# First scores from 256 keys, x's later chunks transposed by DMA, spaced late weights and a rearranged end in a gated attention kernel

## The chip, the core and the metric

One core of a Trainium2 chip runs the kernel. The metric is the device time of one launch in microseconds, the median of several runs; less is better. The engines are TensorE (PE; the profile keeps its weight loads apart as PEld), VectorE (DVE), ScalarE (ACT), GpSimd (POOL) and SyncE (SP, which here only issues DMAs). Each engine takes its instructions in program order and waits at semaphores.

## The reference

All inputs and the output are bf16. S is 2048, D 640, H 32 heads of 20, F 1536.

```python
x = A_x
g = _sigmoid((x * gate_w).sum(-1, keepdims=True))
a = _A_ref(x, A_wqkv, A_wo)             # 32-head softmax attention, then @ wo
b = _B_ref(x, B_w1, B_b1, B_w2)         # (h * tanh(softplus(h))) @ w2 with h = x @ w1 + b1
return g * a + (1 - g) * b
```

## The kernel before

Four heads make a pack, 512 queries a chunk; a pack with a chunk is a group, 32 groups in all. In a group each of 16 key tiles (128 keys) gives four score tiles of 128x512, one per head, computed by four row strips of PE (`score`). A step `S2,0` in the text issues two such tiles into two banks of PSUM, `x` the exponential of them on ACT (two or three tiles in one instruction). A key tile can instead be taken by DVE: `d` takes it, `D` issues one of its four score tiles, and `power_of` (L556) makes the exponential as an integer shift of bits; POOL makes two shifted copies of the finished set (L586), so that such a key tile takes three PV steps where an exponential of ACT takes one (a variant, `two`, takes two). A PV step `V` is four matmuls into the accumulator bank. `normalise` divides at the end of a group, through a transpose on DVE.

Everything else is cut into chains: products that are run in pieces (`C` begins a chain, `F` runs one piece) between the blocks of scores, with an evacuation (`y`) on DVE. Chains make the transposes of x (`transpose_chain`), K of the first pack (`first_k_chain`), the other Q and K (`dense_chain`), V (`v_chain`), the MLP and the final projection (`wo_chain`). The text `ORDER` is the program order of all this, written out by hand for all 32 groups; the numbers behind `C` count chains sorted by their due times, so the text changes wherever the chains do. Other letters: `q`, `k`, `b`, `o` loads that SP issues, `p` POOL's shifts, `m` the Mish activation, `H` four matmuls without effect on the result, `e` the gate, `v` the scaled copies of V.

At the head, x's chunk 0 comes in four DMAs (L444), two from SP and two from ACT. PE transposes it (L1159), the copies out of PSUM go to DVE and ACT in turn (L1165, L1167). The weights of the first pack's Q and K are padded from 20 to 32 columns per head by DVE (`pad_copy`, L500); into the 12 free columns of K's weights goes `w_top` (L1171), so that the first pack's K product also makes the last columns of K for `store_top`. One fill matmul (L1175) follows. Then K and Q of chunk 0 are computed, 512 columns each (L1184), and copied out (L1194, L1192), and the ordered text begins. SP's queue holds, in this order, x chunk 0, the K weights, w_top, x chunk 1, the gate's weights, x chunk 2, a weight strip, x chunk 3, a strip, `wv`, b1, w1, two strips, w1, all of w2, and then what the text issues.

At the end, the four row tiles of the last query chunk are finished in PSUM: pack 6, then a product with the identity that adds what lies in `R`, then pack 7 when `normalise` has its output; copies and DMAs out follow.

Of the kernel before, what the change touches and what calls it, by code (L numbers as in the profile page):

```python
# [9 lines left out]
P = 128  # L10
# [3 lines left out]
BF16 = mybir.dt.bfloat16  # L14
# [5 lines left out]
S2,0 S2,2 C1,6 F x C2,5 F y1 x C3,4 F y2 S2,0 y3 C4,6 F x S3,2 y4 C5,5 F F F F x F F F F F F F F F F F F S2,0  # L20
F F S3,2 x F F C0,6 F F y5 x y6 F y7 F y8 y9 F S2,0 y10 V0,-1 x V1,-1 V2,-1 C6,6 F F F F F V3,-1 C7,5 F y11
C8,4 F y12 S2,0 S2,2 q1 C9,6 F y13 x C10,5 F y14 C11,4 F F x F F y15 F S2,0 F F F F x F F F S2,2 F F F F x F
S2,0 S2,5 F F F x y16 C12,3 F y17 y18 F y19 F y20 F x S3,0 F V4,-1 x V5,-1 y21 V6,-1 C13,6 F S3,3 y22 C14,2 F
x S2,0 y23 C15,6 F C16,2 F x y24 S3,3 y25 V7,-1 C17,6 F x F F F F F F F F F S2,0 F F F F x F S3,2 F F F F F
C18,5 F x F y26 y27 F y28 S2,0 y29 y30 F F x S2,2 y31 V8,-1 V9,-1 x V10,-1 d1,0,1 S2,0 S2,4 d1,1,0 D1,15,0,6
d1,2,0 d1,3,0 x C19,3 F y32 F F F x S3,0 D1,15,3,6 F y33 V11,-1 x S2,4 y34 C20,6 F F F F F F F F F F F x F
S3,0 D1,14,0,3 F F F y35 F F x F F F S2,4 y36 C21,3 F y37 y38 F y39 y40 e0 F v0 y41 F x S3,0 D1,15,1,6 q2 y42
V12,-1 y43 F V13,-1 x V14,-1 y44 S2,4 D1,14,3,6 C22,3 F y45 F F x F S2,0 D1,15,2,2 V15,-1 y46 F x F F S2,4
D1,13,0,6 y47 F p1,4 F F x C23,2 F F y48 F S2,0 F y51 F x S2,4 D1,13,3,6 y52 F y49 F y50 F F F x V0,-1 S2,0
D1,14,1,3 V1,-1 y53 x p2,-1 V15,0 S2,4 y55 C24,6 F y56 x F y57 F S2,0 D1,14,2,2 y54 d1,4,0 F x S2,3 D1,12,0,5  # L30
y58 F V2,-1 y59 x V15,1 p3,5 S2,0 D1,13,1,2 y60 V3,-1 V14,0 x y61 p4,0 S2,3 D1,12,3,5 C25,6 V14,1 y62 F x S2,0
D1,13,2,2 d2,1,0 F y63 F x S3,3 F p5,5 F x V4,-1 S2,0 D1,12,2,2 y64 V14,2 V13,0 y65 V5,-1 p6,0 x V13,1 S3,3
D1,12,1,6 d2,5,0 V6,-1 y66 C26,2 F x F F V13,2 F S2,0 D1,11,0,6 p7,2 F F y67 F x F q3 S2,3 D1,11,1,5 p8,0
V12,0 y68 F F x S2,0 D1,11,3,6 V7,-1 y69 V12,1 y70 x V12,2 y71 S2,2 D1,11,2,5 D2,15,1,4 d2,0,0 V8,-1 y72 x
C27,6 F F S2,0 F y73 p9,2 F F x F S2,2 D2,15,2,5 F F y74 F p10,3 F x S2,0 D2,15,0,4 V11,0 y75 V9,-1 y76 x
V11,1 y77 S2,2 D2,14,1,6 D2,14,2,5 V11,2 y78 x V10,-1 S2,0 D2,15,3,4 d2,2,0 y80 C28,6 F x F S2,2 y79 V0,-1 x
y81 F S2,0 D2,14,0,5 F y82 p11,3 y83 F x S2,2 D2,13,1,4 V1,-1 y85 V15,0 p12,4 x S2,0 D2,14,3,5 y86 d2,6,0
V15,1 C29,6 F y87 x F S2,2 D2,13,2,4 V15,2 y84 F F x y88 p13,1 F S2,0 D2,13,0,5 F F y89 F x F S2,2 D2,12,1,4
p14,3 F V2,-1 y90 V14,0 x S2,0 D2,13,3,5 y91 d3,4,0 C30,4 F F y92 F x F y93 F S2,2 D2,12,2,6 F F y94 F x F
S2,0 D2,12,0,5 V3,-1 y95 F x V14,1 S2,2 D2,11,1,6 y96 p15,1 V14,2 y97 V4,-1 x y98 S2,0 D2,12,3,5 d3,3,0 V13,0  # L40
y99 V5,-1 x S3,2 D2,11,2,6 p16,-1 V13,1 y100 V6,-1 x V12,0 p17,1 S2,0 D2,11,0,5 V13,2 y101 C32,6 F F p18,0 x F
S3,2 D2,11,3,5 d3,5,0 F y102 x F V7,-1 V12,1 y103 S2,0 D3,15,1,5 p19,1 V12,2 y104 V8,-1 x S3,2 D3,15,0,6 V11,0
p20,0 y105 V11,1 x S2,0 D3,15,2,5 V9,-1 y106 C31,6 F F F x S3,2 D3,14,1,5 V11,2 y107 F x F S2,0 y108 V10,-1
# [12 lines left out]
D4,12,3,6 y156 F F x V7,-1 V8,-1 S2,0 y157 H p34,-1 V13,0 y158 x S3,2 D5,15,0,6 C46,5 F y159 F x F F S2,0
D4,12,2,6 F y160 V13,1 x V9,-1 S2,2 D4,12,1,4 y161 d5,1,0 V10,-1 C48,6 F x y162 S2,0 D5,15,2,5 F y163 p35,2 F
x S2,2 D5,15,1,4 V11,-1 y164 F x p36,4 S2,0 D5,15,3,5 d5,5,0 F y165 d5,6,1 V12,0 x V12,1 S3,2 y166 p37,0 V12,2
x C47,5 F S2,0 D5,14,0,6 y167 F p38,2 F y168 F x F y169 S3,2 y170 V0,-1 V15,0 x S2,0 D5,14,1,6 y171 V15,1 q7
q8 y172 V1,-1 V15,2 C49,5 F x S3,2 D5,14,3,6 F y173 F x F F S2,0 D5,14,2,6 y174 d6,0,0 V2,-1 V3,-1 x S3,2 y175  # L60
D5,13,0,5 C50,6 F p39,2 x y176 F F F F S2,0 D5,13,2,5 y177 p40,3 V4,-1 x V14,0 y178 S3,2 D5,13,1,6 V14,1 y179
V5,-1 x S2,0 D5,13,3,5 d6,1,0 V14,2 y180 C51,6 F F F x S3,2 D5,12,2,5 p41,2 F y181 F x V6,-1 V13,0 p42,3 y182
S2,0 D5,12,0,5 V13,1 y183 C52,6 F x S2,2 D5,12,3,4 F y184 F x F S2,0 D5,12,1,5 d6,2,0 F y185 x V7,-1 S3,2
V13,2 y186 p43,4 V8,-1 x S2,0 D6,15,1,5 V9,-1 y188 C53,6 F F F x y187 S3,2 D6,15,0,5 q9 F F x S2,0 y189 V10,-1
p44,-1 V12,0 y190 C54,5 F F x F S2,2 D6,14,0,4 V11,-1 y191 F x F S2,0 D6,15,2,6 y192 V12,1 C55,4 F y193 x S2,2
D6,14,1,5 F y194 F x S2,0 D6,15,3,6 y195 d6,3,0 F F y197 x V0,-1 S2,2 D6,13,0,5 y198 V1,-1 p45,4 x V15,0 S2,0
D6,14,2,6 y199 C56,4 F p46,5 y200 F x S2,2 D6,13,1,5 F y196 y201 F x S2,0 D6,14,3,6 d6,0,0 F y202 V15,1 x y203
# [1273 lines left out]
```

## Time and profile before

| | us |
|---|---|
| runs shown (median, lowest, highest) | 696.98, 696.91, 697.25 |
| profiled execution, its own time | 697.02 |
| span in the profile | 695.2 |
| granted TensorE clock, mean | 0.998 |
| first score matmul, first exponential starts | 10.04, 10.47 |
| last exponential starts | 685.67 |
| DMA traffic | 40.46 MB |

The page of the profile gives busy times by engine, the chain of work that ended last, and groups of instructions. A line in order of time reads: start, length, engine, line of the program, operation, output <- input, shape, count, and in brackets the idle time before it and what ended that. A matmul's length includes the way through the array, so matmuls that follow each other overlap in it.

### The profile page before, as it was taken

The numbers are of one execution on the slowest core, as the hardware profiler recorded it, in microseconds if no ns is written. First come the engines' busy times: TensorE is split into PE (matmuls) and PEld (weight loads), VectorE is DVE, ScalarE is ACT, GpSimd is POOL, SyncE is SP. The second block draws the span as 40 slices with busy tenths as digits, with TensorE's granted clock in tenths as the row PEclk, the third lists the DMA queues.
The fourth block names the chain that finished last, engine by engine and source line by source line (L and its number), as shares of the span: only waits on it lengthen the run. The fifth ranks groups of instructions, "written<-read, shape, count | busy, mean of one in ns | idle before, by whom it ended". The sixth has DMA issues, their size and how long they took to land.

```text
span 695.2 us, 24441 instructions
## 1 busy us (share of the span) xinstructions
PE 680.5 (98%) x10325; PEld 240.0 (35%) x10325; DVE 582.0 (84%) x1009; ACT 676.6 (97%) x665; POOL 339.6 (49%) x334
## 2 busy tenths in 40 slices
PE   8999999999999999999999999999999999999997
PEld 4433333332323343333333222222234333343333
DVE  4488868888799888788898999988989988888896
ACT  5899999999999999999999999999999999999996
POOL 5025443435365434544547555554643565545543
PEclk9999999999999999999999999999999999999999
DMA  9612132313211212112031214232222121143221
GB/s 249 194 15 46 32 75 52 58 51 85 50 26 33 67 37 40 27 38 56 24 83 36 43 32 90 44 67 57 37 63 81 22 50 29 41 74 61 58 58 48
DMA packets 125613, 40.46 MB, mean 58 GB/s; under 512 B 91136, under 2 KB 124944, under 8 KB 125504
## 3 DMA queue, kind: packets, MB, share of 16 engines
q1 hardware_dynamic: 123904, 38.38, 24.7%
q8 instruction: 80, 1.31, 0.8%
q10 hardware_dynamic: 1600, 0.53, 0.3%
q14 instruction: 29, 0.24, 0.1%
HBM read 23.61 MB, written 12.79 MB: 52 GB/s over the span
## 4 chain that ended last, share of the span: by engine, by line
PE 78%; ACT 15%; DVE 3%; issue 3%; DMA 1%; SPq 0%; DVEq 0%; ACTq 0%
PE Sp L1033 26%; PE Sp L1068 26%; PE Sp L633 24%; ACT E L1051 11%; ACT big L840 3%; DVE T L556 2%; DMA w_top<-in_A_wqkv_dram 1%; PE Sp L1284 0%; ACT L1051 0%; PE Sp L1184 0%; DVE VD L538 0%; DVE big L819 0%; DVE T L1111 0%; PE Sp L643 0%; DVE bt L864 0%
## 5 line engine op out<-in xcount | busy, mean ns | idle before, releaser
L1051 ACT ACTIVATE E<-Sp 128x1024 bf16<-128x1024 f32 (+1 forms) x650 | 645.5, 1175 | 5.1 <-PE Sp L1033 4.0
L586 POOL INT64_ADD T<-T x320 | 330.4, 1043 | 340.6 <-DVE T L556 195.8
L556 DVE TENSOR_SCALAR T<-Sp 128x512 int16<-128x512 f32 x640 | 425.0, 685 | 76.9 <-PE Sp L1033 67.3
L1033 PE MATMUL Sp<-qT,kT 32*128 32x512 bf16 x2048 | 260.4, 383 | 6.2 <-ACT E L1051 3.0
L1033 PEld LDWEIGHTS <-kT 32*128 32x128 bf16 x2048 | 71.5, 91 | 240.5 <-issue 236.0
L1068 PE MATMUL Sp<-E,VA 128*21 128x512 bf16 x1408 | 133.9, 383 | 0.0
L1068 PE MATMUL Sp<-T,VD 128*21 128x512 bf16 x1252 | 117.4, 382 | 0.2
L633 PE MATMUL Sp<-w_sb,big 128*32 128x320 bf16 x1536 | 74.2, 301 | 0.6 <-DVE T L556 0.5
L633 PE MATMUL Sp<-xT,w1t 128*32 128x512 bf16 x960 | 73.4, 383 | 0.2
L1068 PEld LDWEIGHTS <-VA 128*21 128x21 bf16 x2048 | 45.5, 90 | 63.3 <-issue 54.2
L1068 PE MATMUL Sp<-T,VA 128*21 128x512 bf16 x640 | 62.4, 381 | 0.0
L633 PE MATMUL Sp<-xT,ws 128*32 128x512 bf16 x720 | 52.3, 381 | 0.2 <-ACT E L1051 0.2
L633 PEld LDWEIGHTS <-big 128*32 128x32 bf16 x1536 | 35.0, 95 | 28.0 <-issue 19.6
L1068 PEld LDWEIGHTS <-VD 128*21 128x21 bf16 x1252 | 30.8, 90 | 39.1 <-issue 32.7
L819 DVE TENSOR_SCALAR big<-Sp,b1f 128x512 bf16<-128x512 f32 x48 | 35.6, 741 | 1.5 <-PE Sp L633 1.1
L633 PE MATMUL Sp<-wv,xT 128*32 128x81 bf16 (+2 forms) x960 | 33.3, 257 | 0.4 <-DVE st L721 0.2
L633 PE MATMUL Sp<-wo_sb,od 128*32 128x320 bf16 (+1 forms) x608 | 28.9, 301 | 0.6 <-DVE T L556 0.6
L633 PEld LDWEIGHTS <-w1t 128*32 128x32 bf16 x960 | 20.1, 95 | 26.3 <-issue 19.4
L721 DVE CAST st<-Sp 128x512 bf16<-128x512 f32 x36 | 24.7, 685 | 5.3 <-PE Sp L633 5.2
L633 PEld LDWEIGHTS <-xT 128*32 128x32 bf16 x960 | 19.1, 96 | 12.8 <-issue 9.2
L777 DVE CAST VA<-Sp 128x80 bf16<-128x80 f32 (+2 forms) x48 | 16.2, 373 | 8.2 <-PE Sp L633 8.2
L633 PEld LDWEIGHTS <-ws 128*32 128x32 bf16 x720 | 16.8, 95 | 17.7 <-issue 10.0
(75 smaller groups left out, 206.1 us busy)
## 6 DMA issues: line engine op xcount, KB each, us to landing
w1t<-in_B_w_dram SPq DMA_DIRECT2D x24, 320.0 KB
q_dram<-st SPq DMA_DIRECT2D x20, 128.0 KB
b_dram<-bt SPq DMA_DIRECT2D x16, 160.0 KB
bl<-b_dram SPq DMA_DIRECT2D x16, 160.0 KB
out_dram<-ot SPq DMA_DIRECT2D x16, 160.0 KB
qT<-q_dram SPq DMA_DIRECT2D x124, 20.0 KB
o_dram<-T SPq DMA_DIRECT2D x120, 20.0 KB
kT<-k_dram SPq DMA_DIRECT2D x28, 80.0 KB
```

Source lines behind the costliest of these rows:

```text
L556: nc.vector.tensor_scalar(out=dst.bitcast(I16), in0=src, scalar1=inv_sqrt_dh * LOG2E * 128.0, scalar2=127.0 * 128.0 + (BETA2 if two else B ...
L586: nc.gpsimd.int64_add(dst[:, :].bitcast(I64), src[:, :].bitcast(I64), n * 0x0001000100010001)
L633: nc.tensor.matmul(out_[k : k + 32], lhsT=lhsT[:, k : k + 32], rhs=rhs, tile_position=(0, k), **kw)
L721: nc.vector.tensor_copy(out=res["st"][:, :], in_=ps[:, :])
L777: nc.vector.tensor_copy(out=VA[:, sts[i], h0 : h0 + nh, 0:DH], in_=ps[:, i, 0:n].rearrange("p (h d) -> p h d", d=DH),)
L819: nc.vector.tensor_scalar(out=big[:, pair_of(c, ft), (ft % 2) * QC : (ft % 2 + 1) * QC], in0=ps[:, :], scalar1=b1f[:, ft : ft + 1], scalar ...
L840: nc.scalar.activation(v, v, ACT.Mish)
L1033: nc.tensor.matmul(ps_cols, lhsT=kT[p][32 * t_ : 32 * t_ + 32, j * P : (j + 1) * P], rhs=qT[G][32 * t_ : 32 * t_ + 32, :], tile_position=( ...
L1051: nc.scalar.activation(E[:, x : x + n, :], allb[:, k0 : k0 + n, :], ACT.Exp, scale=inv_sqrt_dh,)
L1068: nc.tensor.matmul(acc[32 * t_ : 32 * t_ + DH + 1, :], lhsT=lhsT, rhs=rhs, start=(pv_done[G] == 0), stop=(pv_done[G] == pv_total[G] - 1), ...
```

## The change

- Head: the Q weights are loaded by SP and the K weights by ACT's queue (exchanged). Both pad copies go to ACT, after its copy of tile 1, which is now its only one of four. w_top goes into K's weights only after the first products. K of the first 256 keys alone is computed before the scores; Q is computed for 384 and 128 queries. K of chunk 0 is computed again for all 512 keys as a chain at the start of the text, with w_top in place; its evacuation comes in two parts. The fill matmul is gone.
- x's chunks 2 and 3 are no longer loaded and transposed by PE, but transposed by five DMAs each that SP issues. Eight transpose chains are gone.
- The second strips, b1 with w1's first parts, and w2 in six parts are issued by ten steps `l` in the text instead of at the head.
- The text: 646 exponentials (550 of two tiles, 96 of three) instead of 650 (542, 108); 165 key tiles on DVE instead of 160, two of them in group 0, which had none; 836 PV steps instead of 825; one heat step instead of three; 330 shifts on POOL instead of 320. 648 blocks of scores in both. Due times of the first chains move.
- The end: three of the last eight projection evacuations (`LATE`) are made by ACT as a multiplication; what DVE added there comes in by three more identity products. The last two projection chains stand behind the last PV step. The last products go in two pairs of row tiles, and the copies out are one of 640 columns per row tile, two on ACT and two on DVE, with one of the DMAs from ACT's queue.

```diff
-    load_first(1, nc.sync)
-    load_first(0, nc.scalar)
+    load_first(0, nc.sync)
+    load_first(1, nc.scalar)
...
+    def load_xt(c):
+        for kt in range(KT):
+            nc.sync.dma_start(
+                out=xT[:, kt, c * QC : (c + 1) * QC],
+                in_=x2d[c * QC : (c + 1) * QC, kt * P : (kt + 1) * P],
+                transpose=True,
+            )
...
-    load_x(2)
     load_strip(0, 0, nc.sync)
-    load_x(3)
+    load_xt(2)
     load_strip(1, 0, nc.sync)
+    load_xt(3)
     nc.sync.dma_start(out=wv[:, :, :], in_=wrows[:, :, 2 * D : 3 * D])
-    nc.sync.dma_start(b1bf, B_b1.rearrange("(ft p) -> p ft", p=P))
-    load_w1(0)
-    load_strip(0, 1, nc.sync)
-    load_strip(1, 1, nc.sync)
-    load_w1(1)
-    nc.sync.dma_start(out=w2_sb[:, :, :], in_=B_w2.rearrange("(ft p) c -> p ft c", p=P))
+    w2rows = B_w2.rearrange("(ft p) c -> p ft c", p=P)
+
+    def load_late(i):
+        if i < 2:
+            load_strip(i, 1, nc.sync)
+        elif i < 4:
+            if i == 2:
+                nc.sync.dma_start(b1bf, B_b1.rearrange("(ft p) -> p ft", p=P))
+            load_w1(i - 2)
+        else:
+            ft = slice(2 * (i - 4), 2 * (i - 4) + 2)
+            nc.sync.dma_start(out=w2_sb[:, ft, :], in_=w2rows[:, ft, :])
...
+            parts = [(AHEAD, QC), (0, AHEAD)] if c == 0 else [(0, QC)]
+            return [(lambda x=x: copy(*x)) for x in parts], lambda: store_top(c)
...
+                    if (u, half) in LATE:
+                        nc.scalar.mul(out=o, in_=ps[:, :], mul=g_t[:, s : s + 1])
+                        return
...
-        if u == 0:
-            pad_copy(nc.vector, wkp, w_first[1][:, :, :])
-        if u == 2:
-            nc.vector.tensor_copy(
-                out=wkp[:, :, :, DH:32], in_=w_top[:, :, :].rearrange("p k (h d) -> p k h d", h=4)
-            )
-    for k in range(NFILL):
-        nc.tensor.matmul(
-            acc[:, :], lhsT=warm_z[:, 0:P], rhs=warm_z[:, :], start=True, stop=True
-        )
-    pad_copy(nc.vector, wqp, w_first[0][:, :, :])
+        if u == 1:
+            pad_copy(wqp, w_first[0][:, :, :])
+            pad_copy(wkp, w_first[1][:, :, :])
...
+    most, ahead, last = slice(0, QC - P), slice(0, AHEAD), slice(QC - P, QC)
+    nc.scalar.copy(out=qT[0][:, most], in_=first_product(1, wqp, most))
+    nc.vector.tensor_copy(out=kT[0][:, ahead], in_=first_product(4, wkp, ahead))
+    nc.vector.tensor_copy(out=qT[0][:, last], in_=first_product(5, wqp, last))
+    nc.vector.tensor_copy(
+        out=wkp[:, :, :, DH:32], in_=w_top[:, :, :].rearrange("p k (h d) -> p k h d", h=4)
+    )
...
+    order = [(u, p) for p in list(wo_pad)[:-1] for u in range(NU)]
+    for pair in ((0, 1), (2, 3)):
+        order += [(u, p) for p in (None, NQ - 1) for u in pair]
...
+    finish(0, nc.scalar.copy, nc.sync)
+    finish(1, nc.vector.tensor_copy, nc.sync)
+    finish(2, nc.scalar.copy, nc.scalar)
+    finish(3, nc.vector.tensor_copy, nc.sync)
```

More of the change, by code (lines that the diff above doesn't have):

```diff
@@ L438 @@
         flat[:, c * NU * D : (c + 1) * NU * D].rearrange("p (u d) -> p u d", d=D)
-        for c in range(NQC)
+        for c in range(TRC)
     ]
@@ L882 @@
     R = {}
+    LATE = ((2, 1), (3, 0), (3, 1))
     LQ = NQC - 1
@@ L1190 @@
             )
[L1191 to L1194 removed]
+        return ps
+    most, ahead, last = slice(0, QC - P), slice(0, AHEAD), slice(QC - P, QC)
[5 more added lines that the diff above has]
+    )
     for p in range(NQ - NSB, NQ):
@@ L1280, in rest @@
         if p is None:
-            lhsT, rhs = ident[:, :], R[LQ][:, u, cols]
-        else:
-            lhsT, rhs = o_last[p][:, u * P : (u + 1) * P], wo_pad[p][:, cols]
-        nc.tensor.matmul(
-            places[u][half][:, 0:HALF], lhsT=lhsT, rhs=rhs, start=p == NQ - NSB, stop=p == NQ - 1,
-            skip_group_check=True,
-        )
-    for p in (*list(wo_pad)[:-1], None):
-        for u in range(NU):
-            for half in range(2):
-                rest(u, half, p)
-    for u in range(NU):
+            parts = [(ident[:, :], R[LQ][:, u, cols])]
@@ new lines, in rest @@
+            if (u, half) in LATE:
+                parts.append((ident[:, :], bl[NU * LQ + u][:, cols]))
+        else:
+            parts = [(o_last[p][:, u * P : (u + 1) * P], wo_pad[p][:, cols])]
+        for lhsT, rhs in parts:
+            nc.tensor.matmul(
+                places[u][half][:, 0:HALF], lhsT=lhsT, rhs=rhs, start=p == NQ - NSB,
+                stop=p == NQ - 1, skip_group_check=True,
+            )
+    order = [(u, p) for p in list(wo_pad)[:-1] for u in range(NU)]
+    for pair in ((0, 1), (2, 3)):
+        order += [(u, p) for p in (None, NQ - 1) for u in pair]
@@ L1294 @@
+    for u, p in order:
         for half in range(2):
-            rest(u, half, NQ - 1)
+            rest(u, half, p)
     ots_ = [work.tile([P, D], BF16, tag=f"T{u}", name="ot") for u in range(NU)]
     rows_ = [out2d[(NU * LQ + u) * P : (NU * LQ + u + 1) * P, :] for u in range(NU)]
-    for u in range(2):
-        nc.scalar.copy(
-            out=ots_[u][:, :].rearrange("p (a c) -> p a c", a=2), in_=(tx, ty)[u][:, 0:2, 0:HALF]
-        )
-        nc.sync.dma_start(out=rows_[u], in_=ots_[u][:, :])
```

605 lines of the change are left out of this document (307 added, 298 removed).

## The prediction

> **What bounds the kernel now.** I read the head of the page first, then its chain, then busy time by stretch, then the first 45 us and the last 10 us in order of time.
>
> ```profile
> span 695.2 us, 24441 instructions
> PE 680.5 (98%) x10325; PEld 240.0 (35%) x10325; DVE 582.0 (84%) x1009; ACT 676.6 (97%) x665; POOL 339.6 (49%) x334
> PE 78%; ACT 15%; DVE 3%; issue 3%; DMA 1%; SPq 0%; DVEq 0%; ACTq 0%
> ```
>
> Two engines are full, TensorE (PE) and ScalarE (ACT), and the chain changes between them. A microsecond taken from one alone is worth less than one. The stretches (PE busy, PEld, DVE, ACT, POOL, clock, DMA share, GB/s) show where there is air:
>
> ```profile
> 10.00:20.00 10.00, 9.04 (x192) 5.18 (x192) 4.64 (x13) 7.60 (x8) 5.97 (x8) 1.00 1.07 264
> 20.00:30.00 10.00, 9.09 (x226) 5.19 (x224) 4.28 (x13) 9.97 (x10) 0.00 (x0) 1.00 0.81 261
> 30.00:40.00 10.00, 9.16 (x196) 3.59 (x197) 4.78 (x15) 10.00 (x12) 0.00 (x0) 1.00 0.17 50
> 40.00:60.00 20.00, 19.60 (x325) 7.26 (x322) 17.04 (x34) 19.77 (x21) 8.27 (x8) 1.00 0.21 32
> 60.00:200.00 140.00, 139.34 (x2030) 45.65 (x2026) 116.12 (x196) 139.48 (x136) 61.80 (x60) 1.00 0.25 54
> 200.00:237.00 37.00, 36.98 (x502) 10.88 (x503) 36.06 (x60) 36.79 (x40) 19.94 (x20) 1.00 0.18 36
> ```
>
> From 20 to 40 ACT never stops, PE has holes and DVE is half idle: group 0 gives no score tile to DVE, so ACT paces it. PE's holes from 10 to 60 sum to 0.96 + 0.91 + 0.84 + 0.40 = 3.1 us. That is a floor: the scores at 10.04 are booked for 0.40 us though the next block starts at 10.37 (both rows stand below), so short waits are hidden in "busy". After 60 only 0.66 us in 140 is open. So the change can gain in the first 60 us and at the end, hardly between.
>
> ```profile
> 2.11 4.62 DMA w_top<-in_A_wqkv_dram
> 3.74 2.34 PE L1159 MATMUL Sp<-ident,big 128*128 128x128 bf16 x20
> 5.64 0.27 DVE L500 COPY wkp<-wf 128x400 bf16<-128x400 bf16 x1 [0.63 <-DMA wf<-in_A_wqkv_dram]
> 5.05 0.69 ACT L1165 COPY xT<-Sp 128x640 bf16<-128x640 bf16 x1 [0.78 <-PE Sp L1159]
> 5.83 0.48 DVE L1167 COPY xT<-Sp 128x640 bf16<-128x640 bf16 x1
> 7.03 1.25 PE L1184 MATMUL Sp<-xT,wkp 128*128 128x512 bf16 x5 [0.53 <-DVE wkp L1171]
> 9.40 0.59 ACT L1192 CAST qT<-Sp 128x512 bf16<-128x512 f32 x1 [2.59 <-PE Sp L1184]
> 10.04 0.40 PE L1033 MATMUL Sp<-qT,kT 32*128 32x512 bf16 x4 [0.67 <-ACT qT L1192]
> 10.47 7.38 ACT L1051 ACTIVATE E<-Sp 128x1024 bf16<-128x1024 f32 x7 [0.48 <-PE Sp L1033]
> 19.78 20.21 ACT L1051 ACTIVATE E<-Sp 128x1024 bf16<-128x1024 f32 x19 [1.94 <-PE Sp L1033]
> ```
>
> The start hangs on the landing of w_top at 6.73, then ten 512-column products, a copy, the scores. ACT begins exponentials at 10.47 and stands still for 1.94 us before 19.78, when the 16 score tiles of key chunk 0 are used up.
>
> **The change part by part.**
>
> *Head.* w_top is no longer needed first. The Q weights' copy moves to ACT behind its only transpose copy (5.05 + 0.69 = 5.74). Its length, 400 elements from SBUF on ACT, no row shows; the nearest are 0.59 for 512 and 0.69 for 640 elements, so 0.83 ns an element and about 0.49; bounds 0.27 (DVE's copy of the same 400) and 0.69. Q ready at 6.23, K at 6.72. PE's transposes end at 6.08 (3.74 + 2.34) as before. DVE's copy of the third tile, at 5.83 behind the pad copy, can start about 0.2 sooner and is done by 6.1, the fourth tile's by 6.6. PE then does five products each of 384, 256 and 128 columns. At 1.25 us less the 0.39 of the last, a 512-column step is 0.215, so 0.81 + 0.54 + 0.27: PE ends at 7.85. The last evacuations are 256 and 128 columns on DVE, some 0.42 and 0.28 (0.69 for 512, 0.49 for 320 in the kernel's casts). With 0.2 from product to copy, scores start at 8.8 to 8.9 and exponentials at 9.3: **1.2 us** earlier. Bounds: 1.5, and -0.3 if the products run at the half rate of the first rows:
>
> ```profile
> 1.21 2.74 PE L493 MATMUL Sp<-qT 128*128 128x512 bf16 x6 [1.21 <-DVE qT L478]
> 5.88 0.63 PE L1175 MATMUL Sp<-qT 128*128 128x512 bf16 x1
> ```
>
> Six in 2.74 with 0.63 for each is a step of 0.42, double. The fill matmul at 5.88 was still slow, the products at 7.03 were fast. The fill is removed; 7.5 steps of 512 at 0.42 instead of 0.215 cost 1.5 us.
>
> *Group 0.* ACT's rate, 7.38 us for the 16 tiles before the stop, is 0.46 per 128x512 tile; the 16 tiles now end at 9.3 + 7.4 = 16.7. PE reaches the ninth issue of scores behind K chunk 0 for all 512 keys, four transposes, the V product of chunk 0, K chunk 1 and four PV steps, with DVE's five V copies ahead of its K copy. I put the end of K chunk 1's copy at 17.8 and the next exponential at 18.25: a stop of 1.55 instead of 1.94, 0.4 less beside the head's gain. Group 0 then gives 8 tiles to DVE (d0 twice) where before gave none: 8 x 0.46 = 3.7 us less for ACT. PE cannot give all of that back, as it has its own work. What it can give back are its holes: 3.1 us by the rows, more below the bookkeeping. I take **3.3 us**, bounds 0 (ACT waits for PE wherever it was ahead) and 4.1 (0.4 + 3.7, all of ACT's).
>
> *PE's work.* The new order has 11 more PV steps (six more key tiles of the kind on DVE that takes three PV instead of one, one fewer of the kind that takes two) and two fewer heat steps:
>
> ```profile
> 679.57 0.61 PE L1068 MATMUL Sp<-T,VD 128*21 128x512 bf16 x8
> 680.44 0.40 PE L1068 MATMUL Sp<-E,VA 128*21 128x512 bf16 x4
> 10.37 1.01 PE L643 MATMUL Sp<-ident,big 128*128 128x128 bf16 x15
> 11.86 0.45 PE L643 MATMUL Sp<-ident,big 128*128 128x128 bf16 x5
> 17.28 1.25 PE L633 MATMUL Sp<-xT,wkp 128*32 128x512 bf16 x20
> ```
>
> A PV step is 0.61 - 0.40 = 0.21: +2.3 and -0.4. A transpose is (1.01 - 0.45)/10 = 0.056; 40 of them go to the DMA: -2.2. K chunk 0 again is five steps of 0.215: +1.1. Blocks of scores, which cost a switch each, stay at 648. Net **+0.8 us** on PE.
>
> *ACT and DVE.* 20 score tiles go from ACT to DVE.
>
> ```profile
> L1051 ACT ACTIVATE E<-Sp 128x1024 bf16<-128x1024 f32 (+1 forms) x650 | 645.5, 1175 | 5.1 <-PE Sp L1033 4.0
> L556 DVE TENSOR_SCALAR T<-Sp 128x512 int16<-128x512 f32 x640 | 425.0, 685 | 76.9 <-PE Sp L1033 67.3
> L651 DVE COPY xT<-Sp 128x640 bf16<-128x640 bf16 x12 | 5.4, 486 | 3.0 <-PE Sp L643 2.8
> ```
>
> 645.5 us over 1408 tiles is 0.458: ACT loses 9.2 us, and 5.5 of it falls after group 0. DVE gains 20 x 0.685 = 13.7 and loses 8 x 0.486 = 3.9. After 60 us PE has no room, so ACT's slack buys only PE's hidden waits for it: **-0.7 us**, bounds 0 and -3 (the chain's ACT share is mostly that exchange).
>
> *DMA queue.* SP issues ten transposes ahead of wv instead of two plain loads. The trace has the same form, 128x512, from o_dram:
>
> ```profile
> L890 SPq DMA_TRANSPOSE od<-o_dram x19: 1129/1218/2159, 489.1 to 660.2; - x19
> 489.05 5.12 SPq L890 DMA_TRANSPOSE od<-o_dram  x4
> 638.23 5.93 SPq L890 DMA_TRANSPOSE od<-o_dram  x4
> 494.00:496.00 2.00, 2.00 (x29) 0.53 (x25) 1.75 (x4) 2.00 (x3) 1.90 (x3) 1.00 0.33 74
> 496.00:498.00 2.00, 2.00 (x30) 0.57 (x31) 1.92 (x5) 2.00 (x3) 1.60 (x2) 1.00 0.00 0
> ```
>
> At 1.28 us each (5.12/4), landed within 1.8 us of the last issue (traffic is gone by 496), five from 5.4 end at 11.8 and land by 13.6. With a strip load of 0.5 between, the next five land by 20.5. PE meets K chunk 2 at about 17.9 and K chunk 3 from 21.0 to 22.0, by ACT's rate up to the 25th tile. Both are hidden, the second by a microsecond. At 1.48 (5.93/4) it lands at 22.5, half a microsecond late; behind it in PE's queue stand the scores of tile 26 and all of ACT. Cost 0, with 7.3 as the bound at 2.16 each. By the Trainium skill (DMA: Bandwidth & Descriptors, Latency and other measured facts) a DMA transpose moves 261 GB/s, which would be half a microsecond for 128 KB, so this would be no limit at all; the rows show two and a half times that, and the rows are used.
>
> The late weights, w1 and w2 among them, leave the first 30 us, where the DMA share is 0.8 to 1.07, and go between output writes; their first users are groups away, so nothing.
>
> *Tail.*
>
> ```profile
> 687.00 0.40 PE L1068 MATMUL Sp<-T,VD 128*21 128x512 bf16 x4
> 688.43 1.25 PE L1284 MATMUL Sp<-big,ident 128*128 128x320 bf16 x8
> 689.58 1.40 PE L1284 MATMUL Sp<-wo,O 128*128 128x320 bf16 x8
> 690.68 1.29 DVE L1308 CAST ot<-Sp 128x320 bf16<-128x320 f32 x3 [0.47 <-PE Sp L1284]
> ```
>
> Two projection chains move behind the last PV, eight steps of 0.135, and cover DVE's normalisation there. Three more identity products (0.4) come in, seven of them between the halves of the last product, so PE ends 0.3 later after the moved work is taken off. One 640-wide copy (about 0.82) after it replaces the train of three: 0.2 less, and one DMA issue less ahead of the last. The skipped DVE evacuations cost ACT three times some 0.44 after its last exponential. Together **-0.1**, bounds -0.8 and +0.8.
>
> Sum against the profiled execution, 697.02 us (span 695.2 and 1.8 around it; 0.04 over the median of 696.98): 697.0 - 1.2 - 3.3 + 0.8 - 0.7 - 0.1 = **692.5 us**.
>
> **The rivals.**
>
> *Chunk 3 late (slower).* If ten transposes next to wv and x's chunk 1 take over 1.9 us each, K chunk 3 holds PE more than the 4.5 us gained. At 2.16 it lands at 29.3, 7.3 late: 699.8. For it: the DMA share of 1.07 early on, which those rows at 489 did not have. Against: w1 and w2 are gone from that stretch, and 2.16 was the longest of 19. Chance 0.11.
>
> *DVE becomes the bound (slower).* From 200 to 237 DVE is busy 36.06 of 37. If all 9.8 us more on DVE showed there: 692.5 + 9.8 = 702.3; half, 697.4. Against: DVE has 113 us free overall and group 0 and 8 now take tiles or drop them where it is idle. Chance 0.06, at 700.
>
> *Cold products.* Without the fill, products stay at the slow step: 692.5 + 1.5 = 694.0. For it: the fill was in place just before the rate doubled. Against: six warming matmuls and twenty transposes stand unchanged ahead. The Trainium skill (TensorE: Matmul & The Clock Gate, Part 4) says that transposes don't count as busy for the clock, which speaks for this rival; the transposes at 3.74 to 6.08 did run slow here, at 2.34/20, while the first products after the fill ran fast. Chance 0.18.
>
> *Nothing refills.* ACT's freed time waits for PE, and only the head counts: 697.0 - 1.2 + 0.8 = 696.6. Chance 0.07.
>
> *Both engines loosen.* All of group 0's 4.1 and 3 in the steady part, the tail left out: 697.0 - 1.2 - 4.1 + 0.8 - 3 = 689.5. For it: ACT, the engine that group 0 waits for, loses 9.2. Against: PE's holes there are 3.1 by the rows. Chance 0.12.
>
> **How the numbers follow.** 692.5 has 0.46, its own range is 690.5 to 695.2. About 0.2% (1.4 us) is what a measurement of this kernel can tell from no change. Faster by more: 0.46 + 0.18 + 0.12 = 0.76, plus 0.02 for the part of "nothing refills" below 695.6; same 0.05; slower the two rivals, 0.17. The range 689.3 to 698.8 cuts the lowest 0.05 and the worst of the slow ones, about 0.13.
>
> **What would show it.** First exponential at 9.3 (10.6 if the products were cold, visible as a step of 0.32 in the 384-column ones). ACT's idle time before the ninth exponential near 1.5 us, and none before the 13th; a wait of PE for a DMA into xT there is the late chunk. PE's holes from 9 to 60 under 1.5 us by the stretches. ACT under 670 us busy and PE within 1 us of 681. DVE at 592. Wrong if PE's busy share from 60 on falls, or if the gain does not stand by 60 us already.

## The result and the profile after

| | us |
|---|---|
| kernel before, median (11 runs) | 697.08 |
| changed kernel, median (11 runs) | 695.43 (693.88 to 696.72) |
| ratio, 95% interval | 0.9972, 0.996 to 0.9985 |
| profiled execution of the changed kernel, its span | 696.7, 694.6 |

Faster, by 1.65 us; 4.5 were forecast. 695.43 lies inside the range of 689.3 to 698.8, just outside the 690.5 to 695.2 around 692.5. The profiled execution is the second longest of the eleven, so its rows may show more stops than the median run has.

The head first, ACT in order of time (start, length, engine, line, operation, count, in brackets the idle time before and its cause), changed kernel:

```profile
9.32 7.64 ACT L1088 ACTIVATE E<-Sp 128x1024 bf16<-128x1024 f32 x8 [1.18 <-PE Sp L1070]
18.47 1.94 ACT L1088 ACTIVATE E<-Sp 128x1024 bf16<-128x1024 f32 x2 [1.51 <-PE Sp L1070]
27.61 2.00 ACT L1088 ACTIVATE E<-Sp 128x1024 bf16<-128x1024 f32 x2 [2.07 <-PE Sp L1070]
45.04 1.45 ACT L1088 ACTIVATE E<-Sp 128x1536 bf16<-128x1536 f32 x1 [1.86 <-PE Sp L1070]
```

The first exponential stands at 9.32 and the idle time before the ninth is 1.51, as forecast. Then come two stops of two microseconds that the kernel before did not have. Engine by stretch (length, PE busy, PEld, DVE, ACT, POOL, clock, DMA share, GB/s), changed kernel:

```profile
10.00:20.00 10.00, 9.52 (x200) 4.91 (x196) 4.62 (x13) 8.39 (x10) 5.20 (x6) 1.00 0.60 105
20.00:30.00 10.00, 7.70 (x227) 3.48 (x219) 4.34 (x15) 7.04 (x7) 0.00 (x0) 0.87 0.56 136
30.00:40.00 10.00, 9.75 (x189) 3.62 (x190) 8.83 (x17) 9.64 (x11) 2.08 (x2) 0.96 0.19 55
40.00:60.00 20.00, 18.27 (x266) 6.44 (x266) 15.90 (x31) 17.06 (x17) 9.39 (x10) 0.91 0.37 55
60.00:686.00 626.00, 622.65 (x9383) 214.43 (x9381) 546.52 (x914) 622.01 (x612) 330.82 (x319) 1.00 0.25 54
```

The last of these stretches in the kernel before:

```profile
60.00:686.00 626.00, 620.95 (x9318) 212.07 (x9318) 541.62 (x902) 623.50 (x611) 321.18 (x312) 1.00 0.23 50
```

PE's holes from 10 to 60 grew from 3.1 to 4.8 us (0.48 + 2.30 + 0.25 + 1.73) where under 1.5 was forecast, and the clock, 1.00 in all of these stretches before, is 0.87 to 0.96 from 20 to 60. After 60 the holes shrank from 5.05 to 3.35. So the change wins where little was hoped for and loses where its main gain was to be. By these rows the gain does not stand by 60 us, which the forecast had named as a sign of being wrong. What PE waited for at the two stops and between them, in order of time, changed kernel:

```profile
23.75 0.40 PE L661 MATMUL Sp<-xT,wkp 128*32 128x512 bf16 x4
25.97 0.40 PE L661 MATMUL Sp<-xT,wkp 128*32 128x512 bf16 x4 [1.82 <-DMA xT<-in_A_x_dram]
36.95 0.37 PE L1070 MATMUL Sp<-qT,kT 32*128 32x512 bf16 x1 [0.25 <-DMA qT<-q_dram]
43.55 0.37 PE L1070 MATMUL Sp<-qT,kT 32*128 32x512 bf16 x1 [1.73 <-DVE T L584]
```

SP's queue in the same kernel (start, length, line, kind, output <- input, count):

```profile
5.52 7.88 SPq L463 DMA_TRANSPOSE xT<-in_A_x_dram  x5
14.07 8.32 SPq L463 DMA_TRANSPOSE xT<-in_A_x_dram  x5
23.14 2.56 SPq L1237 DMA_DIRECT2D o_dram<-wo  x4
25.81 6.58 SPq L717 DMA_DIRECT2D k_dram<-kT  x12
34.59 1.39 SPq L778 DMA_DIRECT2D qT<-q_dram  x4
```

The first stop is x's chunk 3: its five transposes held SP's queue for 8.32 us, and PE could go on with it at 25.97. The second is DVE, which stood behind the gate. Between them lies a wait of 0.25 us for group 1's queries. What SP issues behind the transposes is later: the kernel before issued that load at 31.15, and its four stores of zeros into o_dram at 19.83 instead of 23.14:

```profile
19.83 3.22 SPq L1202 DMA_DIRECT2D o_dram<-wo  x4
31.15 1.40 SPq L749 DMA_DIRECT2D qT<-q_dram  x4
```

DVE at the second stop, changed kernel, in order of time; the gate's first instruction waits for ACT, and two scaled copies of V follow before DVE gets to the score tile whose bank PE needs:

```profile
40.96 0.17 DVE L1244 TENSOR_SCALAR g_t<-g_t 128x16 f32<-128x16 f32 x1 [0.96 <-ACT g_t L1243]
41.54 1.36 DVE L566 TENSOR_SCALAR VD<-VA 128x588 bf16<-128x588 bf16 x2
42.83 0.67 DVE L584 TENSOR_SCALAR T<-Sp 128x512 int16<-128x512 f32 x1
```

The gate is not all of this stop. The second of the two copies took 1.12 us beside two shifts of POOL (41.62 to 43.85), where the first took 0.33 and both together took 0.56 in the kernel before, whose gate stood in the same place while POOL was idle. So about 0.8 of the 1.73 us lies in that copy.

### The profile page after: what moved, and what is told of

It reads as the page before. It is cut to its first block, busy times and chain, and to the rows that moved or that the text cites. A ratio compares the mean times of both kernels' runs of the same rounds, so it can differ in the third digit from the quotient of the medians.

```text
span 694.6 us, 24521 instructions
## 1 busy us (share of the span) xinstructions
PE 680.7 (98%) x10348; PEld 240.5 (35%) x10348; DVE 589.5 (85%) x1018; ACT 671.0 (97%) x664; POOL 352.1 (51%) x345
## 4 chain that ended last, share of the span: by engine, by line
PE 80%; ACT 10%; DVE 3%; SPq 3%; issue 2%; DMA 2%; ACTq 0%; DVEq 0%
PE Sp L1105 27%; PE Sp L1070 27%; PE Sp L661 25%; ACT E L1088 8%; SPq L463 2%; ACT big L869 2%; DVE T L584 1%; DMA xT<-in_A_x_dram 1%; DMA q_dram<-st 1%; DMA big<-in_A_x_dram 1%; PE Sp L1322 1%; SPq L1181 0%; ACT L1088 0%; DVE VD L566 0%; DVE T L1134 0%
## 5 line engine op out<-in xcount | busy, mean ns | idle before, releaser
L1088 ACT ACTIVATE E<-Sp 128x1024 bf16<-128x1024 f32 (+1 forms) x646 | 638.3, 1169 | 12.9 <-PE Sp L1070 10.9
L614 POOL INT64_ADD T<-T x330 | 342.3, 1049 | 327.8 <-DVE T L584 165.7
L584 DVE TENSOR_SCALAR T<-Sp 128x512 int16<-128x512 f32 x660 | 438.1, 684 | 77.1 <-PE Sp L1070 66.7
L1105 PE MATMUL Sp<-E,VA 128*21 128x512 bf16 x1388 | 132.4, 384 | 0.0
L1105 PE MATMUL Sp<-T,VD 128*21 128x512 bf16 x1296 | 123.3, 383 | 0.0
L1105 PE MATMUL Sp<-T,VA 128*21 128x512 bf16 x660 | 64.1, 382 | 0.4 <-DVE T L584 0.4
L661 PEld LDWEIGHTS <-w1t 128*32 128x32 bf16 x960 | 21.5, 95 | 24.5 <-issue 17.2
L1134 DVE STREAM_TRANSPOSE T<-Sp 128x512 f32<-128x512 f32 x32 | 22.6, 706 | 0.5 <-PE Sp L1105 0.4
```

The source lines that it names most:

```text
L584: nc.vector.tensor_scalar(out=dst.bitcast(I16), in0=src, scalar1=inv_sqrt_dh * LOG2E * 128.0, scalar2=127.0 * 128.0 + (BETA2 if two else B ...
L614: nc.gpsimd.int64_add(dst[:, :].bitcast(I64), src[:, :].bitcast(I64), n * 0x0001000100010001)
L661: nc.tensor.matmul(out_[k : k + 32], lhsT=lhsT[:, k : k + 32], rhs=rhs, tile_position=(0, k), **kw)
L1088: nc.scalar.activation(E[:, x : x + n, :], allb[:, k0 : k0 + n, :], ACT.Exp, scale=inv_sqrt_dh,)
L1105: nc.tensor.matmul(acc[32 * t_ : 32 * t_ + DH + 1, :], lhsT=lhsT, rhs=rhs, start=(pv_done[G] == 0), stop=(pv_done[G] == pv_total[G] - 1), ...
L1134: nc.vector.transpose(out=st["T1"][:, :, :].rearrange("p b r -> p (b r)"), in_=acc[:, :])
```

## The experiments

All kernels compute the whole result. Each was timed beside the kernel before, whose median was 697.19 beside the first four, 697.24 beside the next four and 697.43 beside the last four. The first theories were T1, the late chunk 3, and T2, the gate in DVE's queue. The edits of the text show single steps out of longer lines; what stands around them is left out.

**K chunk 3's product behind work that needs chunks 0 to 2.** The order of the text alone:

```diff
-C10,6 F F y15 y16 F y17 S2,0 y18 y19 S3,2 F x F V4,-1 V5,-1 y20 x C11,5 F F F F F F F F F F
+y15 y16 S2,0 y17 y18 y19 S3,2 C11,5 F F F F F F F F F F x V4,-1 V5,-1 F F F F F F F F F F x
+S2,0 y20 y21 x S2,2 C10,6 F F F F F x
...
```

> The product of K chunk 3 stands behind the scores and the V product of the tiles that need only chunks 0 to 2; nothing else is changed, and its DMA transposes come as before. Theory 1 (the gain of the head is lost where PE waits for the last DMA transpose of x: 1.82 us by the row at 25.97, ACT idle 2.07 before 27.61, then 3.4 us at half clock): PE's wait for a DMA into xT near 26 falls under 0.3 us, no half clock before 40 us, 1.5 to 2.5 us less than the changed kernel. Rival (PE or ACT would have waited there anyway for something else, or the wait comes out later): within 0.5 us of the changed kernel.

**The gate later.** It moves to where group 1 is well under way, and one evacuation goes ahead of the copies of V:

```diff
-y44 e0 S3,2 D1,14,3,5 v0,0 y46 F y47 F y45
+y44 S3,2 D1,14,3,5 v0,0 y45 F y46 F y47
...
+e0 l2
```

> The gate's exponential and its three DVE operations stand some 20 us later in the text, and one DVE evacuation stands ahead of the two scaled copies of V instead of behind them; K chunk 3 is late as in the changed kernel. Theory 2 (the second stop, PE 1.73 us before 43.55 and ACT 1.86 before 45.04, comes from DVE waiting for ACT's gate exponential and doing 1.27 us of scaled copies ahead of the evacuation that PE needs): that wait falls under 0.4 us and the half clock near 44.5 goes, 1 to 2 us less than the changed kernel. Rival (that stop only catches up what the late chunk had shifted): within 0.5 us of it.

**Chunks 2 and 3 transposed by PE**, loaded plainly, with DVE's copies out of PSUM (steps `t` in the text, 40 transposes):

```diff
-    load_xt(2)
+    load_x(2)
...
-    load_xt(3)
+    load_x(3)
```

> x's chunks 2 and 3 are loaded plainly and transposed by PE as in the kernel before, 40 transposes with eight DVE copies put between the steps of the text; everything else is the changed kernel. Theory 1: no wait for a DMA near 26, PE works 2.2 us more for the transposes, and SP is free some 12 us sooner; with the wait of 1.8 us and the half clock gone the time is 0 to 1.5 us less than the changed kernel. Rival (the transposes by DMA are hidden and worth their PE time, the wait costs little): 1.5 to 2.5 us more than the changed kernel.

**The first two edits together.**

> K chunk 3 later and the gate later together. Theories 1 and 2 together: both waits gone, clock full from 7 to 690 us, 2.5 to 4.5 us less than the changed kernel, near 692. If one stop only stands in for the other: no better than the better of the two alone by more than 0.5 us.

| | median | lowest to highest (runs) | ratio, interval |
|---|---|---|---|
| K chunk 3 later | 695.53 | 693.77 to 696.35 (7) | 0.9972, 0.996 to 0.9983 |
| gate later | 696.64 | 693.97 to 697.97 (10) | 0.9986, 0.9973 to 0.9998 |
| transposes by PE | 697.76 | 696.65 to 698.13 (10) | 1.0002, 0.9993 to 1.0012 |
| both orders | 696.42 | 693.78 to 699.65 (10) | 0.9987, 0.9968 to 1.0006 |

The gain of neither theory came in the medians. K chunk 3 later is within 0.1 us of the changed kernel, as its rival had it, the gate later 1.2 above it, and both orders together no better than the first alone. The transposes by PE are 2.3 above it, inside the 1.5 to 2.5 of their rival. Each edit removed its own stop. With K chunk 3 later the second stop is gone as well, though the gate stands where it was: a wait for group 1's queries comes ahead of it. PE's row there, in order of time:

```profile
37.29 0.37 PE L1070 MATMUL Sp<-qT,kT 32*128 32x512 bf16 x1 [2.00 <-DMA qT<-q_dram]
```

The same with both orders:

```profile
35.87 0.37 PE L1070 MATMUL Sp<-qT,kT 32*128 32x512 bf16 x1 [0.72 <-DMA qT<-q_dram]
```

With the gate later alone, the first stop stays (1.7 us) and PE's other waits up to 62 us are 0.4 or less. Its profiled execution, 694.49, is 2.1 below its median, so no row shows what its longer executions lose.

The stretch from 20 to 30 with the transposes on PE:

```profile
20.00:30.00 10.00, 8.80 (x229) 4.39 (x221) 4.61 (x12) 5.80 (x6) 0.00 (x0) 1.00 0.09 26
```

The load of group 1's queries was 0.25 us late in the changed kernel because PE itself had been held up. With PE on time it is 0.7 to 2.0 late. With the transposes on PE no DMA is late, but ACT works only 5.8 of 10 us there, and the stop behind the gate is still 1.8 us: all 40 transposes on PE cost more than the late DMAs. The four forms of the kernel that wait for SP also spread by 2.6 to 5.9 us from run to run, the one with the transposes on PE by 1.5. That gave theory S: the price of the DMA transposes is SP's queue, and all that stands behind them in it.

**Heat at the two stops**: a heat step in PE's queue ahead of each, to see whether the lost clock is a price of its own.

```diff
-S3,2 F x F V4,-1 V5,-1 y20 x
+S3,2 F x H F V4,-1 V5,-1 y20 x
...
-y48 S2,0 D1,15,1,5
+y48 S2,0 H D1,15,1,5
```

> The changed kernel with two heat steps (four matmuls each that add zeros) in PE's queue, one ahead of the piece of K chunk 3 that waits for the DMA, one ahead of the score tile that waits for DVE behind the gate. Nothing is moved and nothing becomes ready sooner; only the two idle stretches of PE, 1.8 and 1.7 us, get work in their middle. Theory C (each stop costs twice: its own length and then 1.7 us because PE runs 3.4 us at half rate): the half-rate stretches get rare, granted clock 0.998 or more in most runs, median 1.0 to 2.5 us below the changed kernel's 695.4, and the highest run under 696. Theory L (the time is lost to the late data alone, and ACT or the next wait makes up what the clock takes): median within 0.6 us of 695.4, whatever the clock does. If the heat itself costs, 0.2 to 0.9 us more.

695.43 (694.33 to 698.64, 10 runs). The median stays, as theory L (late data alone) had it, but half-rate stretches did not get rare (clocks of 0.993 to 1.0), so theory C (each stop costs twice) is not tested by it: in the profile the wait for the queries, 1.5 us and without heat, now stopped PE.

**SP's four stores of zeros later**, on top of both orders:

```diff
-    for u in range(NU):
-        r0 = LQ * QC + u * P
-        nc.sync.dma_start(
-            out=o_dram[r0 : r0 + P, (NQ - NSB) * HF : D],
...
     def gate_values():
...
                     in_=g_dram[32 * r : 32 * r + 32, NU * LQ : NU * LQ + NU],
                 )
+        for u in range(NU):
+            r0 = LQ * QC + u * P
+            nc.sync.dma_start(
+                out=o_dram[r0 : r0 + P, (NQ - NSB) * HF : D],
...
```

> Both reorderings (K chunk 3's product later, gate later), and SP's four stores of zeros into o_dram moved from behind wv to behind the gate's loads, 2.6 to 3.2 us of SP's queue that stood ahead of all stores of K and Q. Theory S (the ten transposes hold SP until 22 us, so that the store and load of group 1's queries come late and set when group 1 starts): the wait for group 1's queries, 0.7 us in the profile with both reorderings and 2.0 with the first alone, disappears; the load of the first of them is issued 2 to 3 us sooner; median 1 to 2.5 us below that kernel's 696.4 and spread under 3 us. Rival: SP's queue is waiting for PE's K chunk 3 anyway, and the load is issued less than 1 us sooner: median within 0.6 us of 696.4.

693.42 (693.18 to 694.11, 4 runs), ratio 0.9948 (0.9933 to 0.9963): 3.0 below the kernel with both orders. No wait of PE for a DMA is left. SP's queue in that kernel:

```profile
23.46 6.96 SPq L717 DMA_DIRECT2D k_dram<-kT  x12
32.71 1.39 SPq L778 DMA_DIRECT2D qT<-q_dram  x4
```

And in the one with both orders alone:

```profile
22.58 3.16 SPq L1237 DMA_DIRECT2D o_dram<-wo  x4
25.84 5.40 SPq L717 DMA_DIRECT2D k_dram<-kT  x12
33.45 1.39 SPq L778 DMA_DIRECT2D qT<-q_dram  x4
```

In these two profiles the load is only 0.74 us sooner, under the one microsecond of the rival, since the twelve stores of K ahead of it take 6.96 us instead of 5.40; the two executions differ by 0.7 (693.44 and 694.14), the wait that went. The profile of the kernel with both orders is one of its two best runs; the rest of the 3.0 lies in its others, which no row shows.

**Chunk 2 by PE, chunk 3 by DMA, gate later.**

```diff
-    load_xt(2)
+    load_x(2)
...
-y2 C6,5 F y6 F F F F x F F F F F S2,0 F F F x S2,2
+y2 C6,5 F y6 t8,4 F F F F x F F F F F t9,6 S2,0 F F F t10,4 x S2,2
```

> x chunk 2 loaded plainly and transposed by PE again (20 transposes), chunk 3 still by five DMA transposes, gate later. SP's queue is 7 us shorter, PE has 1.1 us more work and DVE four copies more before 25 us. Theory S with late chunk 3: chunk 3 lands by 15 us, no wait of PE for a DMA before group 1, group 1's queries 3 to 5 us sooner: median 692.5 to 694.5. Rival from the run with all transposes on PE: PE is the engine that is short in 10 to 30 us, and half of that loss, about 1.2 us, comes back: median 695.5 to 697.

**692.70** (692.59 to 693.07, 4 runs), ratio 0.9937 (0.9922 to 0.9952), faster than both kernels and the best of all here. SP's queue in it:

```profile
8.40 6.84 SPq L463 DMA_TRANSPOSE xT<-in_A_x_dram  x5
29.85 1.39 SPq L778 DMA_DIRECT2D qT<-q_dram  x4
```

ACT in order of time, one row:

```profile
22.42 24.00 ACT L1088 ACTIVATE E<-Sp 128x1024 bf16<-128x1024 f32 x24 [0.51 <-PE Sp L1070]
```

The first stretches:

```profile
10.00:20.00 10.00, 9.26 (x184) 5.33 (x184) 5.96 (x16) 6.56 (x8) 4.74 (x5) 1.00 0.99 190
20.00:30.00 10.00, 9.55 (x269) 4.28 (x261) 5.83 (x17) 9.49 (x10) 0.00 (x0) 1.00 0.23 62
30.00:40.00 10.00, 9.66 (x212) 4.40 (x212) 8.98 (x20) 10.00 (x11) 2.31 (x3) 1.00 0.30 78
40.00:60.00 20.00, 19.43 (x307) 6.84 (x304) 17.59 (x34) 19.00 (x21) 11.42 (x12) 1.00 0.11 5
```

The load is issued 4.7 us sooner than in the changed kernel, ACT runs 24 us without a stop, PE's holes from 10 to 60 are 2.1 us and the clock is full throughout. Ahead of that row ACT stood still for 2.99 us before the ninth exponential, twice the changed kernel's 1.51, since PE does the transposes there.

**The late weights back at the head**, behind wv, with the DMA transposes kept:

```diff
+    for i in (2, 0, 1, 3, 4, 5, 6, 7, 8, 9):
+        load_late(i)
...
-        "l": load_late,
+        "l": lambda i: None,
```

> The changed kernel, but with the ten late loads (second strips, b1, w1, w2) issued at the head behind wv, as the kernel before had them, and none in the text. SP's queue gets about 8 us longer ahead of the stores of K and Q. Theory S: group 1's queries come 5 to 8 us later and PE stops there: median 699 to 703. Rival (the queue has that much room, and the late loads' place is worth nothing, as the prediction had it): median within 1 us of 695.4.

706.02 (705.3 to 707.26, 4 runs), ratio 1.013 (1.0113 to 1.0147): 10.6 us more than the changed kernel, beyond what S had put (699 to 703). SP's queue in it (its lines count three more):

```profile
28.80 4.88 SPq L489 DMA_DIRECT2D w_sb<-in_B_w_dram  x6
44.70 1.39 SPq L781 DMA_DIRECT2D qT<-q_dram  x4
```

And PE's wait:

```profile
47.18 0.58 PE L1073 MATMUL Sp<-qT,kT 32*128 32x512 bf16 x1 [10.78 <-DMA qT<-q_dram]
```

The load comes 10.1 us later than in the changed kernel (44.70 and 34.59), and the kernel takes 10.6 more. SP's queue had no room there. Not all of the 10.6 is the wait itself: PE's holes from 10 to 60 grow by 8.9, and its clock from 40 to 60 is 0.66.

**Four more on the parts of the best kernel.** Its gate edit taken away; the stores of zeros alone, on the changed kernel; the stores on the best kernel; and chunk 3 instead of chunk 2 on PE.

> Chunk 2 transposed by PE, chunk 3 by DMA, the gate where the change has it: the run with 692.7 less its gate edit. Theory S (SP's queue is the cause, the gate's stop is a second, smaller one that a late group 1 made worse): no wait of PE for a DMA before 60 us; a wait for T behind the gate of 1 to 2 us stays; median 693.5 to 695. Rival (the gate's place is what gave the 692.7): median 695.4 or more, as changed.

> The changed kernel with SP's four stores of zeros moved behind the gate's loads, nothing else. Theory S in its plain form (the load of group 1's queries is the late thing): issued 2 to 3 us sooner, median 1.5 to 3 below 695.4, spread under 1.5 us. Theory of two late things (K chunk 3's transposes land late whatever stands behind them in SP's queue, then the gate): the wait of 1.4 to 1.8 us for x's chunk 3 stays, median within 1 us of 695.4 and the spread of over 2 us stays.

> The run with 692.7 (chunk 2 by PE, gate later) with SP's four stores of zeros moved back as well: two more microseconds for SP's queue. In that run no wait of PE for a DMA is left, so all theories say that nothing is left to gain there: 692.7 within 0.4. If it is faster by more, waits for the queue were hidden below the rows.

> Chunk 2 by DMA, chunk 3 by PE, gate later: SP's queue as short as in the run with 692.7, but the 1.1 us of transposes fall into 18 to 24 us, where PE waits for ACT in the runs without DMA waits, instead of 11 to 18, where ACT waits for PE. Theory S: the same relief, median 691.8 to 692.7. Rival (chunk 2's DMA transposes, the first in the queue, are themselves late or slow the loads of chunk 1): PE waits for x's chunk 2 before 18 us, median 693.5 or more.

| | median | lowest to highest (runs) | ratio, interval |
|---|---|---|---|
| best kernel without the gate edit | 694.28 | 693.86 to 694.92 (4) | 0.9953, 0.994 to 0.9966 |
| stores later, alone | 693.34 | 692.2 to 694.92 (4) | 0.994, 0.9924 to 0.9956 |
| best kernel, stores later | 693.76 | 692.92 to 696.64 (6) | 0.9953, 0.9937 to 0.997 |
| chunk 3 on PE | 694.61 | 694.28 to 695.53 (5) | 0.9958, 0.9945 to 0.9971 |

What PE waited for longest from 9 to 62 us in the first of them (us in total, times, longest):

```profile
PE Sp L1070 <- DVE T L584: 1.8, 1, 1.8
```

And in the last:

```profile
PE Sp L1286 <- DMA big<-in_A_x_dram: 1.9, 1, 1.9
```

The gate edit is worth 1.6 us once SP is relieved (694.28 and 692.70; 1.4 if each is taken against the kernel before beside it), and brought nothing while it was not. In the first of them the second copy of V again takes 1.12 us beside POOL, in the best kernel 0.32; no run moves POOL's shifts alone, so how much of the gate's price is that meeting is open. With chunk 3 on PE its plain load stands behind five DMA transposes in SP's queue and is 1.9 us late: S again, though neither expectation had named it. Moving four small stores is by itself worth 2.1 us on the changed kernel. The load of group 1's queries came 2.2 us sooner, as S had it, but the spread of 2.7 is wider than the 1.5 of S, and its profile still has both stops. So no wait in it locates the 2.1; what the clock has to do with it stands in the last section. On the best kernel the stores gain nothing, as expected, but the median is 1.1 higher, outside the 0.4 allowed; two of six runs are above 695, its profile, the fastest of them, shows no wait for a DMA, and why is open. So the spread is not SP's queue alone.

## Why the forecast was right in sign and wrong in size

- **Head, 1.2 us: right in size, in part by luck.** 10.47 became 9.32, 1.15. "Cold products" came true for two of the fifteen: the 384-column products start at 6.37, 6.66, 6.98 and 7.14, so the first two steps are 0.29 and 0.32, double the 0.16 of the next, and cost 0.3 us instead of 1.5. The clock rose at 6.97, after 3.42 us in which PE was busy for 3.16, most of it the transposes. From then on the steps are fast: five for K of the first 256 keys take 0.71, the last of them 0.27, so 0.11 each, half of the 0.215 for 512. The sum put both last copies behind PE's last product, but K's copy ran beside it, and that gave the 0.3 back. In the later profiles, which run the same head, the first exponential starts anywhere from 8.79 to 9.50.

```profile
6.37 1.26 PE L1214 MATMUL Sp<-xT,wqp 128*128 128x384 bf16 x5 [0.26 <-ACT wqp L520]
7.47 0.71 PE L1214 MATMUL Sp<-xT,wkp 128*128 128x256 bf16 x5
8.21 0.42 DVE L1225 CAST kT<-Sp 128x256 bf16<-128x256 f32 x1 [1.57 <-PE Sp L1214]
```

- **Group 0, 3.3 us: failed**, and this is the term that the result lacks. It assumed that PE can fill its holes with ACT's freed time. In the changed kernel PE could not, because the step **"DMA queue ... cost 0"** was wrong. It took 1.28 us for a transpose, from rows in a quiet stretch. Seven of the ten held the queue for about that (1.25 to 1.26), three for 2.05 to 2.67; what made the three long no run shows. So SP was done with the last at 22.4, not at 18.7, and it landed 3.5 us after that, not 1.8 (chain of the changed kernel: start, length, what):

```profile
21.13 4.80 DMA xT<-in_A_x_dram
```

Chunk 3 let PE go on at 25.97; it was to land at 20.5. PE itself came to it at 24.15, not from 21 to 22, so that 5.4 us of lateness made a stop of 1.8. That is the rival "chunk 3 late" with a price of 1.8 us instead of its 7.3, not enough to make the kernel slower. The larger omission is that the step stopped at the landing. SP issues in order, and behind the transposes stood the zeros, 16 stores of K and the load of group 1's queries. With PE on time that load was the next wait, 0.7 to 2.0 us.

- **"Late weights ... so nothing": wrong.** They had to leave the head for the transposes to go in: behind the transposes at the head they cost 10.6 us. The forecast asked when their users come and not what they hold up.
- **The gate** was not in the forecast at all: 1.4 to 1.6 us when nothing else is late, its meeting with POOL's shifts included.
- **Steady part, 0.7: mis-sized.** PE's holes from 60 to 686 fell by 1.7 (5.05 to 3.35). The forecast read 0.66 in the 140 us from 60 to 200 and found "hardly" any room after 60; the kernel before had 1.32 from 237 to 260 and 1.82 from 514 to 540, and 1.3 of the 1.7 came from there.
- **PE's work, +0.8**: PE was busy 680.7, within the microsecond of 681 that was named, but the row hides the two half-rate stretches; the best kernel has 678.7 with 20 transposes more. So the net work did not grow as forecast, or waits hidden in the booked time went; the rows don't tell which. The engines' busy times, changed kernel, then the best one:

```profile
PE 680.7 (98%) x10348; PEld 240.5 (35%) x10348; DVE 589.5 (85%) x1018; ACT 671.0 (97%) x664; POOL 352.1 (51%) x345
```

```profile
PE 678.7 (98%) x10368; PEld 240.6 (35%) x10368; DVE 590.6 (86%) x1022; ACT 670.4 (97%) x664; POOL 352.3 (51%) x345
```

- **DVE** was forecast at 592 and came to 589.5; "DVE becomes the bound" is false. ACT came to 671.0 where under 670 was said.
- **Tail, -0.1**: from the end of PE's last product to the end of the span the changed kernel takes 3.8 us (694.6 less 690.11 and 0.71), the one before 4.2 (695.2 less 689.58 and 1.40). Some 0.4 instead of 0.2 there; what PE does ahead of it was not taken apart.

```profile
690.11 0.71 PE L1322 MATMUL Sp<-wo,O 128*128 128x320 bf16 x4
```

For the profiled execution, 4.2 us over the forecast (696.7 and 692.5): 3.3 more holes before 60, 3.4 of work lost to two half-rate stretches of 3.41, if each costs half its length, and 1.0 less after 60; the remaining 1.5 in the kernel's favour no row locates. With half of the transposes back on PE and the gate out of the way the forecast's own sum, 692.5 with 20 transposes at 0.056 added, is 693.6, and 692.7 was measured. So the sum of the other terms held within a microsecond, though not each of them, and the queue and the gate took the difference: chunk 2 back on PE alone brought 1.2 of it (695.43 to 694.28), the gate edit the rest.

## What to carry to other kernels

Price a DMA moved to a queue by the time that it holds that queue, and follow the queue to the first transfer behind it that somebody waits for. Where a stop moves when its cause is removed, look for what all of them have in common, here one queue in order, before repairing them one by one. What a step leaves behind when it moves out of a queue has its price too, as the weights showed.

## What the runs showed of the hardware

A DMA transpose of 128x512 held SP's queue for 1.26 us in the median of the ten at the head (1.25 to 2.67) and for 1.22 in the quiet stretch of the kernel before (1.13 to 2.16). The plain loads around them held it for 0.4 to 0.6 us each (rows at 5.11, 13.45 and 22.44). The Trainium skill (DMA: Bandwidth & Descriptors, Rules for kernel authors) says that spreading DMAs over issuing engines only saves the sequencer's issue time; here that time was nearly the whole price, 10.1 us of it for 10.6 us in the run with the weights at the head.

The second copy of V on DVE took 1.12 us beside POOL's shifts in four profiles (the changed kernel, the transposes on PE, the stores alone, the best kernel without the gate edit), and 0.32 to 0.33 in the ten others; the four are the ones with a stop of 1.7 to 1.8 us behind the gate.

A stop of PE of under 2 us can be followed by a half-rate stretch of the clock. Windows of the changed kernel around its two stops:

```profile
24.04:27.45 3.41, 1.59 (x59) 0.92 (x54) 0.69 (x1) 1.50 (x2) 0.00 (x0) 1.00 0.90 280
27.45:30.86 3.41, 3.41 (x61) 1.09 (x58) 2.73 (x8) 2.77 (x3) 0.00 (x0) 0.50 0.15 37
41.10:44.52 3.42, 1.69 (x23) 0.31 (x15) 3.35 (x9) 2.08 (x2) 2.14 (x2) 1.00 0.18 44
44.52:47.93 3.41, 3.41 (x51) 1.47 (x47) 1.52 (x3) 2.05 (x2) 0.00 (x0) 0.50 0.13 6
```

And around the first stop of the kernel with the stores moved alone, which has the same two (2.1 and 1.8 us):

```profile
21.14:24.55 3.41, 1.99 (x49) 0.68 (x35) 0.75 (x5) 3.41 (x4) 0.00 (x0) 1.00 0.65 116
24.55:27.96 3.41, 2.29 (x94) 1.40 (x97) 1.36 (x2) 1.12 (x2) 0.00 (x0) 1.00 0.66 226
```

Changes of the clock lie 3.41 us or whole multiples of it apart. In the changed kernel each stop fell into one such window and left PE busy for 1.6 to 1.7 of it, and the next ran at half rate; in the other kernel the first stop fell across two, with 2.0 and 2.3, and the clock stayed. The other profiles make no threshold of it: windows with 1.27, 1.43, 1.87 and 2.04 were followed by half rate, one with 1.56, of the kernel with chunk 3 on PE, was not. The two spans, 694.6 and 691.4, differ by 3.2, about what two windows at half rate lose (3.4). The Trainium skill (TensorE: Matmul & The Clock Gate, Part 1) has a free-running window of 3413 ns, and the trace agrees; its advice to avoid gaps of over 3 us (Why this matters for your kernels) is too lax here, where 1.7 to 1.8 us were enough. The runs with both orders fit: 693.78 and 694.14 with a mean clock of 1.0 and 0.999, 695.16 to 695.69 with 0.997, 697.16 to 699.65 with 0.995. That the clock alone makes such a spread isn't shown: the run with heat did not keep it up, the changed kernel took 694.79 with 0.994 and 695.43 with 0.998, and the fastest run with the stores alone, 692.2, had 0.996.
